# Attention and gated block in one kernel: narrowing at steps' ends, global work first, four scaling products, a packed transposition less

## The chip, the cores and the metric

The kernel runs on one core of a Trainium2 chip. The metric is the device time of one execution in microseconds (us); lower is better. The core has four compute engines that run their own instruction queues in order: TensorE (PE in the profile, PEld for its weight loads), VectorE (DVE), ScalarE (ACT) and GpSimd (POOL). SyncE (SP) issues most transfers.

## What is computed

The reference is attention, then a gated feed-forward block, then a routed block of 8 experts, all in fp32. Cut to what the change touches:

```python
# batch 4, 8 heads, 512 local and 32 global positions, head_dim 64, window 32
s_g = scale * q_g @ k_all.T            # 32 global queries see all 544 keys
out_g = sm(s_g) @ v_all
s_ll = where(|i - j| <= 32, scale * q_l @ k_l.T, -1e9)
s_l = concat([scale * q_l @ k_g.T, s_ll])   # local queries: 32 global keys and the window
out_l = sm(s_l) @ concat([v_g, v_l])
x = concat([out_g, out_l])             # 2304 tokens of 512
gate = 1 / (1 + exp(-(x @ w_gate)))    # 512 x 1536
x = (gate * (x @ w_val)) @ w_out       # then the routed experts on rows that a score picks
```

## The kernel before

**Attention** runs as a software pipeline of 38 steps over 32 units; unit u is 128 local queries (tile u // 2) of one half g = u % 2 of the heads, and a step does a different stage for several units. The list MAIN gives the order in a step u: scores of the global queries out (u-1), `turn_mm` (u-3), `normalise` (u-2), `score_mm` (u), `turned` (u-3), `x_out` (u-5), the exponentials (u-1), the middle of the step ("mid"), the scores' maxima `score_max` (u), `global_mm` (u), `value_mm` (u-4), and the end of the step ("end"). Each engine's queue is in this written order.

A unit's weights `pr` are 128 x 2 x 320: for each of two pairs of heads two chunks of 160 (128 local keys and 32 global ones). `normalise` divides by the row sums r (128 x 4) and copies the global keys' columns into a packed tile `pk`; `turn_mm` transposes four blocks of 128 and the packed one on TensorE into the tile `tp`; `turned` copies it to `pt`; `value_mm` (L438) multiplies.

**Side work** is put into the middles and ends of steps by tables of (step, stage); a half number is the middle of the step above it. `side` holds the functions for each place, called in the order in which they were put there. G_STEPS (G_LAST for the last batch) lists, from step 8b + 8, the stages of the global queries of batch b for g = 0 and 1: top (maximum), weigh (exponential, ScalarE, L463), over (reciprocal of the sums, VectorE, L467 and L468), norm (the weights `pgf`, 128 x 544, times it; its engine is ENG['g_n']), turn and turned (transposition on TensorE, L477, and copy to `ptg`, L112), value (L491, L492), out.

W_STEPS does the same for five of the twelve weight sets of the gated block. A set is three tiles of 512 KB that come as 64-bit integers: fetch (transfer to `raw`), narrow (three VectorE passes, L164, L166, L168, to fp32), total (ScalarE, L185), sum over partitions (TensorE, L188), scale (VectorE, L178 to L180 and L539), high (ScalarE, L110) and low (VectorE, L210 and L117). X_STEPS splits the tokens of the gated block's first part. W_TAIL does sets 5 and 6 in steps 33 to 36, partly; the rest is in block 0.

**Gated blocks** go over the tokens in BLOCKS of 4, 3, 3, 2, 3, 2 tiles of 128, each over 12 chunks fc of 128 columns: `up` (24 matmuls, L576 to L578), `gated` (sg on ScalarE L587, g on VectorE L589), `cut` (gh on ScalarE, go on VectorE L603) and `down` of the chunk before (L615 to L617). Block 0's first four chunks' `up` run at the ends of steps 33 to 36. Block 0 also makes weight sets 6 to 11: w1_sum, w1_make (scale, high, low, the next transfers) and w1_words (narrows and totals of a later set).

Of the kernel before, what the change touches and what calls it, by code (L numbers as in the profile page):

```python
# [49 lines left out]
G_STEPS = [[(0, 'top'), (0.5, 'weigh'), (1.5, 'over'), (1.5, 'norm'), (2, 'turn', 0), (2.5, 'turned', 0), (3, 'turn', 1), (3.5, 'turned', 1), (4, 'value'), (4.5, 'out')], [(1, 'top'), (1.5, 'weigh'), (2.5, 'over'), (2.5, 'norm'), (5, 'turn', 0), (5.5, 'turned', 0), (6, 'turn', 1), (6.5, 'turned', 1), (7, 'value'), (7.5, 'out')]]  # L50
G_LAST = [[(0, 'top'), (0, 'weigh'), (0.5, 'over'), (0.5, 'norm'), (1, 'turn', 0), (1, 'turned', 0), (1.5, 'turn', 1), (1.5, 'turned', 1), (2, 'value'), (2.5, 'out')], [(0, 'top'), (0, 'weigh'), (0.5, 'over'), (0.5, 'norm'), (2.5, 'turn', 0), (2.5, 'turned', 0), (3, 'turn', 1), (3, 'turned', 1), (3.5, 'value'), (4, 'out')]]
W_STEPS = [(0, 'fetch', 0), (0.5, 'fetch', 1), (2.5, 'narrow', 0), (3, 'total', 0), (3, 'narrow', 1), (3.5, 'fetch', 2), (3.5, 'total', 1), (4, 'sum'), (4.5, 'scale'), (4.5, 'high', 0), (5, 'low', 0), (5, 'high', 1), (5.5, 'narrow', 2), (5.5, 'low', 1), (6, 'high', 2), (6, 'low', 2)]
W_FIRST = (8, 13, 18, 23, 28)

W_TAIL = [(33.5, 'narrow', 15), (34, 'total', 15), (34.5, 'narrow', 16), (35, 'total', 16), (35, 'narrow', 17), (35, 'fetch'), (35.5, 'sum', 5), (36, 'make', 5),
# [5 lines left out]
ENG = {'x': 'a', 'g_n': 'a', 't0': 'a', 't1': 'a', 'tg': 'v'}  # L61
# [19 lines left out]
def moe_kernel(ctx, tc, qL, kL, qG, vA, wpack, epack, wr, wrT, masks, cst, out):  # L81
# [311 lines left out]
    def normalise(u):  # L393
        pr, r = U[u, "pr"], U.pop((u, "r"))
        nc.vector.tensor_scalar(r, r, 1e-9, None, op0=ALU.add)
        nc.vector.reciprocal(r, r)
        r = r.rearrange("q (a c) -> q a c", a=2).unsqueeze(3)
        (st, n), (ca, _), (one, _) = pr.ap
        x = bass.AP(tensor=pr.tensor, offset=pr.offset, ap=[[st, n], [ca, 2], [192 * one, 2], [one, 128]])
# [3 lines left out]
        nc.vector.tensor_tensor(pk.rearrange("q (a c k) -> q a c k", a=2, c=2), pr[:, :, 128:192].rearrange("q a (c k) -> q a c k", c=2),  # L403
                                r.to_broadcast([128, 2, 2, 32]), op=ALU.mult)
# [45 lines left out]
    def globals_(b, g):  # L450
# [310 lines left out]
    def w1_make(n):  # L761
# [11 lines left out]
        w1_words(n + 2 if n >= NWA else n + 1)  # L773
# [53 lines left out]
    for u in range(STEPS):  # L827
# [170 lines left out]
    for n in range(NB):  # L998
# [11 lines left out]
        for fc in range(NFC):  # L1010
            if n or fc >= EARLY:
                up(n, fc)
                gated(n, fc)
                cut(n, fc)
            if n == 0:
# [5 lines left out]
            if n == 0 and fc == 1:  # L1021
                cut(0, 3)
# [389 lines left out]
```

## Time and profile before

| | us |
|---|---|
| median of 3 runs | 815.66 (813.95 to 815.85) |
| profiled execution | 819.66 |
| its span, first to last instruction | 817.9 |
| busy in the span: TensorE / VectorE / ScalarE / GpSimd | 747.9 / 503.2 / 359.1 / 65.4 |
| mean granted clock of TensorE, share of full | 0.961 |

The span is the profiled execution's without the 1.76 us around it. Engines run beside each other, so busy times don't add up. Attention fills the first 180 us or so, the gated blocks the time to about 630 us, the experts the rest.

### The profile page before, as it was taken

What the parts mean: (1) busy time and instruction counts of PE and PEld (TensorE: products, weight loads), DVE (VectorE), ACT (ScalarE), POOL (GpSimd) and SP (SyncE); (2) the same over time, 40 slices, a digit from 0 to 9 for tenths busy, and PEclk for the clock granted to TensorE, in tenths of its full rate; (3) what the DMA queues carried; (4) which work ended last, traced back from release to release, by engine and by line L of the source; (5) the groups of instructions that cost most, each with busy time, mean ns of one, the idle gap of its engine ahead of it and who ended that gap; (6) DMA issues with size and microseconds to landing.
All of it is one profiled execution on the core that took longest, in us unless ns stands there. A gap on an engine that the chain in (4) does not pass through costs nothing. (4 is left out here: it accounts for less than half of the span.)

```text
span 817.9 us, 14475 instructions
## 1 busy us (share of the span) xinstructions
PE 747.9 (91%) x5110; PEld 560.0 (68%) x5110; DVE 503.2 (62%) x1369; ACT 359.1 (44%) x874; POOL 65.4 (8%) x92
## 2 busy tenths in 40 slices
PE   6988888998979999999999999999999866999993
PEld 5877787756545666666678866678787645777772
DVE  6768899768884277546557746336555567763731
ACT  5965887733443322132232232235334465561630
POOL 2000000000000000010010010000303112230200
PEclk9998899999999999999999999999999798999997
DMA  8999997556402210110021010015635567873300
GB/s 229 231 258 254 277 270 214 159 157 220 167 26 103 91 39 1 53 40 26 1 80 39 1 66 26 27 61 185 175 110 166 186 227 240 260 247 104 135 15 18
DMA packets 60360, 106.03 MB, mean 130 GB/s; under 512 B 9185, under 2 KB 31249, under 8 KB 60258
## 3 DMA queue, kind: packets, MB, share of 16 engines
q1 hardware_dynamic: 54242, 94.60, 37.6%
q0 software_dynamic: 3136, 6.73, 2.6%
q10 hardware_dynamic: 2880, 3.41, 1.4%
q8 instruction: 55, 0.90, 0.5%
q14 instruction: 47, 0.39, 0.2%
HBM read 87.84 MB, written 18.12 MB: 130 GB/s over the span
## 5 line engine op out<-in xcount | busy, mean ns | idle before, releaser
L576 PE MATMUL pp<-xh,wa 128*128 128x384 f16 (+2 forms) x576 | 184.3, 320 | 4.3 <-ACT sg L587 4.3
L577 PE MATMUL pp<-xl,wa 128*128 128x384 f16 (+2 forms) x576 | 183.6, 319 | 0.0
L578 PE MATMUL pp<-xh,wa 128*128 128x384 f16 (+2 forms) x576 | 183.4, 318 | 0.0
L589 DVE SCALAR_TENSOR_TENSOR g<-pp,inv,sg 128x384 f32<-128x384 f32 (+2 forms) x72 | 42.8, 594 | 100.9 <-PE pp L578 98.0
L224 DVE TENSOR_TENSOR wb<-raw,wa 128x1024 fp32r<-128x1024 f32 x64 | 76.7, 1222 | 28.7 <-ACT wa L223 27.7
L587 ACT ACTIVATE sg<-pp,inv 128x384 f32<-128x384 f32 (+2 forms) x72 | 40.4, 561 | 119.8 <-PE pp L578 113.1
L602 ACT CAST gh<-g 128x384 fp32r<-128x384 f32 (+2 forms) x71 | 35.0, 494 | 129.3 <-DVE g L589 129.3
L576 PEld LDWEIGHTS <-wa 128*128 128x128 f16 x576 | 56.9, 99 | 44.8 <-issue 16.5
L615 PE MATMUL acc<-wb,gh 128*128 128x512 f32 x200 | 86.5, 433 | 0.2 <-ACT gh L602 0.2
L577 PEld LDWEIGHTS <-wa 128*128 128x128 f16 x576 | 56.6, 98 | 33.5 <-issue 5.7
L617 PE MATMUL acc<-wb,go 128*128 128x512 f32 x200 | 79.3, 397 | 0.0
L578 PEld LDWEIGHTS <-wa 128*128 128x128 f16 x576 | 56.6, 98 | 33.1 <-issue 1.6
L616 PE MATMUL acc<-wb,gh 128*128 128x512 f32 x200 | 79.0, 395 | 0.0
L223 ACT CAST wa<-raw 128x1024 fp32r<-128x1024 f32 x64 | 65.5, 1049 | 27.1 <-DMA raw<-in_epack_dram 25.2
L725 DVE CUSTOM_DVE_ANT_0 junk<-x,wrow 128x512 f32<-128x512 f32 x108 | 75.4, 698 | 2.6
L603 DVE TENSOR_TENSOR go<-g,gh 128x384 fp32r<-128x384 f32 (+2 forms) x71 | 37.9, 534 | 39.1 <-ACT gh L602 39.1
L351 PE MATMUL sp<-k,qz 128*128 128x160 f32 x256 | 47.6, 336 | 8.0 <-DMA qz<-in_qL_dram 5.4
L391 ACT ACTIVATE pr<-sm,st 128x160 f32<-128x160 f32 x128 | 53.0, 424 | 0.0
L351 PEld LDWEIGHTS sp<-k,qz 128*128 128x128 f32 x256 | 41.8, 217 | 9.7 <-POOL tok L274 5.3
L705 POOL DMA_INDIRECT lst<-tok,pi x17 | 17.1, 1009 | 346.0 <-DVE cum L709 342.4
L615 PEld LDWEIGHTS acc<-wb,gh 128*128 128x128 f32 x200 | 37.7, 189 | 9.2 <-ACT gh L602 0.4
L617 PEld LDWEIGHTS acc<-wb,go 128*128 128x128 f32 x200 | 37.6, 188 | 9.0 <-DVE go L603 0.2
(280 smaller groups left out, 1345.3 us busy)
## 6 DMA issues: line engine op xcount, KB each, us to landing
raw<-in_epack_dram SPq DMA_DIRECT2D x64, 512.0 KB
raw<-in_wpack_dram SPq DMA_DIRECT2D x36, 512.0 KB
k<-in_kL_dram SPq DMA_DIRECT2D x32, 256.0 KB
x1d<-x SPq DMA_DIRECT2D x16, 260.0 KB
w<-in_vA_dram SPq DMA_DIRECT2D x32, 128.0 KB
xTd<-xT SPq DMA_DIRECT2D x16, 256.0 KB
out_dram<-x SPq DMA_DIRECT2D x16, 256.0 KB
v<-in_vA_dram SPq DMA_DIRECT2D x12, 256.0 KB
```

Of the source, the lines that this page charges most:

```text
L223: nc.scalar.copy(t[0], raw)
L224: nc.vector.tensor_sub(t[1], raw, t[0])
L351: nc.tensor.matmul(sp[:, 160 - 160 * s:320 - 160 * s], q, qk[t][g][:, pp, 96 * s:96 * s + 160], start=True, stop=True)
L391: nc.scalar.activation(U[u, "pr"][:, c // 2, cs], sm[:, c // 2, cs], AF.Exp, bias=st[:, c:c + 1], scale=-1.0, accum_out=U[u, "r"][:, c:c + 1])
L576: nc.tensor.matmul(pp[:, 0:nt], hi[:, ks], xh[k][:, 0:nt], start=(k == 0), stop=False)
L577: nc.tensor.matmul(pp[:, 0:nt], hi[:, ks], xl[k][:, 0:nt], start=False, stop=False)
L578: nc.tensor.matmul(pp[:, 0:nt], lo[:, ks], xh[k][:, 0:nt], start=False, stop=(k == 3))
L589: nc.vector.scalar_tensor_tensor(g[:, 0:nt], ps[1][:, 0:nt], inv[:, 2 * fc + 1:2 * fc + 2], sg[:, 0:nt], op0=ALU.mult, op1=ALU.mult)
L615: nc.tensor.matmul(acc, gh[:, gs], hi, start=(fc == 0), stop=False)
L616: nc.tensor.matmul(acc, gh[:, gs], lo, start=False, stop=False)
L617: nc.tensor.matmul(acc, go[:, gs], hi, start=False, stop=(fc == NFC - 1))
L725: nc.vector.tensor_tensor_reduce(junk, R["x1"][:, g, 0:DM], wrow[c], op0=ALU.mult, op1=ALU.add, scale=1.0, scalar=0.0, accum_out=R["lo"][: ...
```

## The change

The change moves global and weight stages to other half steps (the tables below) and puts the global stages ahead of other side work in the same place (`first=True`). The global weights are normalised on GpSimd instead of ScalarE. `normalise` uses four products of 128x160 with a per-partition scalar, in place, instead of two with a broadcast operand, and writes no packed tile; `turn_mm` turns the global keys' columns with two matmuls of 64 stationary columns against the identity instead of one packed transposition. `value` computes for each half only the 32 columns that it needs. The sum and the making of set 5 go half a step back, behind `up(0, 3)`; those of set 6 go behind `down(0, 0)`; in block 0 a set's totals and third narrow are put off (list `late`) to between `gated` and `cut` of the next chunk.

```diff
-G_STEPS = [[(0,'top'),(0.5,'weigh'),(1.5,'over'),(1.5,'norm'),(2,'turn',0),(2.5,'turned',0),(3,'turn',1),(3.5,'turned',1),(4,'value'),(4.5,'out')],
-           [(1,'top'),(1.5,'weigh'),(2.5,'over'),(2.5,'norm'),(5,'turn',0),(5.5,'turned',0),(6,'turn',1),(6.5,'turned',1),(7,'value'),(7.5,'out')]]
+G_STEPS = [[(0,'top'),(0.5,'weigh'),(1,'over'),(1.5,'norm'),(2.5,'turn',0),(3,'turned',0),(3.5,'turn',1),(4,'turned',1),(4.5,'value'),(5,'out')],
+           [(1,'top'),(1.5,'weigh'),(2,'over'),(2.5,'norm'),(5.5,'turn',0),(6,'turned',0),(6.5,'turn',1),(7,'turned',1),(7.5,'value'),(8,'out')]]
-W_STEPS = [(0,'fetch',0),(0.5,'fetch',1),(2.5,'narrow',0),(3,'total',0),(3,'narrow',1), ...
-           (5,'low',0),(5,'high',1),(5.5,'narrow',2),(5.5,'low',1),(6,'high',2),(6,'low',2)]
+W_STEPS = [(0,'fetch',0),(1,'fetch',1),(2,'narrow',0),(2.5,'total',0),(3,'narrow',1), ...
+           (5,'low',0),(5.5,'high',1),(6,'low',1),(6,'narrow',2),(6.5,'high',2),(7,'low',2)]
-W_TAIL = [... (35.5,'sum',5),(36,'make',5), ...
+W_TAIL = [... (36,'sum',5),(36.5,'make',5), ...
-ENG = {'x': 'a', 'g_n': 'a', ...
+ENG = {'x': 'a', 'g_n': 'p', ...
...
-    def at(u, f):
+    def at(u, f, first=False):
...
-            side.setdefault(u, []).append(f)
+            side.setdefault(u, []).append((not first, f))
+    def side_work(u):
+        for _, f in sorted(side.get(u, ()), key=lambda x: x[0]):
+            f()
...
-        nc.vector.tensor_tensor(x, x, r.to_broadcast([128, 2, 2, 128]), op=ALU.mult)
-        U[u, "pk"] = pk = apool.tile([128, 128], F32, tag="pk", name="pk", bufs=2)
-        nc.vector.tensor_tensor(pk.rearrange(...), pr[:, :, 128:192].rearrange(...), r.to_broadcast([128, 2, 2, 32]), op=ALU.mult)
+        for c in range(4):
+            x = pr[:, c // 2, 160 * (c % 2):160 * (c % 2) + 160]
+            nc.vector.tensor_scalar(x, x, r[:, c:c + 1], None, op0=ALU.mult)
...
-        nc.tensor.transpose(tp[:, 4], U.pop((u, "pk")), ident)
+        for pp in range(2):
+            nc.tensor.matmul(tp[64 * pp:64 * pp + 64, 4], pr[:, pp, 128:192], ident, start=True, stop=True)
...
             for pp in range(2):
-                for c in range(4):
-                    nc.tensor.matmul(xo[:, pp], v[:, c, 2 * g + pp], pt[:, c, 64 * pp:64 * pp + 64], ...)
-                nc.tensor.matmul(xo[:, pp], v[0:64, 4, 2 * g + pp], pt[0:64, 4, 64 * pp:64 * pp + 64], ...)
+                for c in range(5):
+                    k = slice(0, 128 if c < 4 else 64)
+                    for j in range(2):
+                        hs, o = slice(64 * j, 64 * j + 64), 64 * pp + SG * j
+                        nc.tensor.matmul(xo[hs, pp], v[k, c, 2 * g + pp, hs], pt[k, c, o:o + SG], ...)
...
+        def rest():
+            if n < NW:
+                for k in range(3 * n, 3 * n + 2):
+                    total_w1(k)
+                narrow_w1(3 * n + 2)
...
+                while late:
+                    late.pop()()
                 cut(n, fc)
-            if n == 0:
+            if n == 0 and fc:
                 w1_sum(W_MAKE.get(fc, NW))
...
             if n == 0 and fc == 1:
+                w1_sum(W_MAKE[0])
+                w1_make(W_MAKE[0])
                 cut(0, 3)
```

The new lines lie up to 4 further down in the attention and 1 in the gated block (L395 is L399, L467 is L468, L578 is L579).

What this moves is seen in three places of the engines' queues. The first is VectorE in the attention around step 10, where the first tile of the first weight set (step 8 on) is narrowed. In the rows, out<-in are tiles: `pr` a unit's weights, `r` its row sums, `cut` and `raw` the narrowing, `gt` the global sums, `sm` the masked scores, `ptg` the turned global weights. Before:

```order
L400 TENSOR_TENSOR pr<-pr,r 128x2x2x128
L403 TENSOR_TENSOR pk<-pr,r 128x128
L164 TENSOR_SCALAR cut<-raw 128x512
L166 SCALAR_TENSOR_TENSOR cut<-raw,cut 128x512
L168 SCALAR_TENSOR_TENSOR raw<-raw,cut 128x512
L112 COPY ptg<-tpg 128x512
L467 TENSOR_SCALAR gt<-gt 128x1
L468 RECIPROCAL gt<-gt 128x1
L362 ISA sm,st<-sp,mask_sb 128x160
```

And after the change:

```order
L468 TENSOR_SCALAR gt<-gt 128x1
L469 RECIPROCAL gt<-gt 128x1
L164 TENSOR_SCALAR cut<-raw 128x512
L166 SCALAR_TENSOR_TENSOR cut<-raw,cut 128x512
L168 SCALAR_TENSOR_TENSOR raw<-raw,cut 128x512
L399 TENSOR_SCALAR r<-r 128x4
L400 RECIPROCAL r<-r 128x4
L403 TENSOR_SCALAR pr<-pr,r 128x160 x4
L366 ISA sm,st<-sp,mask_sb 128x160
```

The narrowing (L164 to L168) stood behind the normalising and ahead of the copy to `ptg` and of `over` (L467, L468); now it stands behind `over` and ahead of the normalising and of the maxima (L362, now L366), and the copy comes a step's maxima later.

The second is VectorE in block 0, in a chunk from 4 on. `g` and `go` are the chunk's, `wa` and `wb` the low parts of a set, `cut` and `raw` the narrows of a later one. Before:

```order
L589 SCALAR_TENSOR_TENSOR g<-pp,inv,sg 128x512
L603 TENSOR_TENSOR go<-g,gh 128x512
...
L210 SCALAR_TENSOR_TENSOR wa<-raw,ws,wa 128x512 x2
L117 TENSOR_TENSOR wb<-raw,wb 128x512
L164 TENSOR_SCALAR cut<-raw 128x512 x2
L166 SCALAR_TENSOR_TENSOR cut<-raw,cut 128x512 x2
L168 SCALAR_TENSOR_TENSOR raw<-raw,cut 128x512 x2
L164 TENSOR_SCALAR cut<-raw 128x512
L166 SCALAR_TENSOR_TENSOR cut<-raw,cut 128x512
L168 SCALAR_TENSOR_TENSOR raw<-raw,cut 128x512
L589 SCALAR_TENSOR_TENSOR g<-pp,inv,sg 128x512
```

And after the change:

```order
L590 SCALAR_TENSOR_TENSOR g<-pp,inv,sg 128x512
L164 TENSOR_SCALAR cut<-raw 128x512
L166 SCALAR_TENSOR_TENSOR cut<-raw,cut 128x512
L168 SCALAR_TENSOR_TENSOR raw<-raw,cut 128x512
L604 TENSOR_TENSOR go<-g,gh 128x512
...
L210 SCALAR_TENSOR_TENSOR wa<-raw,ws,wa 128x512 x2
L117 TENSOR_TENSOR wb<-raw,wb 128x512
L164 TENSOR_SCALAR cut<-raw 128x512 x2
L166 SCALAR_TENSOR_TENSOR cut<-raw,cut 128x512 x2
L168 SCALAR_TENSOR_TENSOR raw<-raw,cut 128x512 x2
L590 SCALAR_TENSOR_TENSOR g<-pp,inv,sg 128x512
```

Of the three narrows behind the lows the third has moved into the next chunk, between `g` and `go`.

The third is TensorE at the end of step 36 and the start of block 0. `pp` is the result of `up` (here its last matmul of chunk 2, and `up` of chunk 3 where `wa` follows), `tpg` a turned block of global weights, `ws` a set's sum, `xog` the global values, `acc` the result of `down`. Before, from the last matmul of chunk 2:

```order
L578 MATMUL pp<-xh_1970,wa 128x512
L477 MATMUL tpg<-ident,pgf_107 128x128
L188 MATMUL ws<-vm,onesf 128x2
L491 MATMUL xog<-ptg,v_109 128x64 x4
L492 MATMUL xog<-ptg,v_109 128x64
...
L578 LDWEIGHTS wa
L578 MATMUL pp<-xh_1970,wa 128x512
L188 MATMUL ws<-vm,onesf 128x2
L615 MATMUL acc_2806<-wb,gh 128x512
L616 MATMUL acc_2806<-wb,gh 128x512
```

After the change, from the last matmuls of chunk 3:

```order
L578 MATMUL pp<-xl_2058,wa 128x512
L579 LDWEIGHTS wa
L579 MATMUL pp<-xh_2057,wa 128x512
L188 MATMUL ws<-vm,onesf 128x2
L616 MATMUL acc_2908<-wb,gh 128x512
L617 MATMUL acc_2908<-wb,gh 128x512
L618 MATMUL acc_2908<-wb,go 128x512
...
L617 MATMUL acc_2911<-wb,gh 128x512
L618 MATMUL acc_2911<-wb,go 128x512
L188 MATMUL ws<-vm,onesf 128x2
L616 MATMUL acc_2908<-wb,gh 128x512
```

The first `ws` is the sum of set 5: it stood ahead of `up` of chunk 3 and now stands behind it. The second `ws` in each is the sum of set 6: it stood ahead of the first `down` and now stands behind it.

## Rows read from the trace of the kernel before

**Rows 1.** Table of stretches: busy us (instructions), TensorE's granted clock, DMA share, GB/s.

```profile
16.00:30.00 14.00, 13.55 (x213) 12.21 (x213) 9.81 (x55) 12.17 (x52) 0.00 (x0) 1.00 1.08 252
30.00:151.00 121.00, 102.92 (x1342) 93.73 (x1341) 100.95 (x406) 92.55 (x323) 0.00 (x0) 0.92 0.88 247
47.68:50.68 3.00, 3.00 (x11) 2.63 (x12) 2.90 (x14) 2.70 (x8) 0.00 (x0) 0.50 1.08 324
```

**Rows 2.** TensorE's waits from 30 to 250 us: total, times, longest.

```profile
PE tpg L477 <- ACT pgf L110: 4.9, 2, 3.4
PE pp L576 <- ACT sg L587: 4.3, 2, 2.4
PE tpg L477 <- DVE ptg L112: 3.9, 3, 3.3
```

**Rows 3.** Timeline of TensorE in an early step: start, duration.

```profile
24.99 0.53 PE L374 MATMUL gp<-k,qg 128*64 128x128 f32 x8
25.34 0.32 PE L438 MATMUL xo<-pt,v 128*64 128x64 f32 x4
...
26.07 0.29 PE L438 MATMUL xo<-pt,w 128*64 128x64 f32 x4
26.19 0.29 PE L438 MATMUL xo<-pt,g 128*64 128x64 f32 x4
26.41 0.66 PE L411 MATMUL tp<-ident,pr 128*128 128x128 f32 x4
26.90 0.27 PE L412 MATMUL tp<-ident,pk 128*128 128x128 f32 x1
27.01 0.30 PE L351 MATMUL sp<-k,qz 128*128 128x160 f32 x1
```

**Rows 4.** Timeline of TensorE over a global unit's values.

```profile
110.58 1.10 PE L491 MATMUL xog<-ptg,v 128*128 128x64 f32 x8
111.61 0.43 PE L492 MATMUL xog<-ptg,v 64*128 64x64 f32 x2
111.97 1.10 PE L491 MATMUL xog<-ptg,v 128*128 128x64 f32 x8
```

**Rows 5.** Timeline of VectorE's normalising; last, VectorE's groups, 16 to 151 us.

```profile
14.84 0.69 DVE L400 TENSOR_TENSOR pr<-pr,r 128x512 f32<-128x512 f32 x1
15.44 0.29 DVE L403 TENSOR_TENSOR pk<-pr,r 128x128 f32<-128x128 f32 x1
15.64 0.32 DVE L362 CUSTOM_DVE_ANT_0 sm<-sp,mask_sb 128x160 f32<-128x160 f32 x1
...
L539 DVE TENSOR_SCALAR inv<-we,xq 128x2 f32<-128x2 f32 x4 | 0.8, 221 | 0.0
```

**Rows 6.** Timeline of VectorE and TensorE around the longest wait.

```profile
45.15 0.43 DVE L164 TENSOR_SCALAR cut<-raw 128x512 uint32<-128x512 uint32 x1 [4.16 <-DMA raw<-in_wpack_dram]
...
47.68 0.48 PE L477 MATMUL tpg<-ident,pgf 128*128 128x128 f32 x1 [3.71 <-DVE gt L467]
```

**Rows 7.** Groups of ScalarE, 16 to 200 us, and of GpSimd, whole span.

```profile
L110 ACT ACTIVATE pgf<-pgf,gt 128x544 f32<-128x544 f32 x8 | 5.9, 746 | 6.2 <-DVE gt L468 6.2
...
L1005 POOL MEMSET zrows<- 128x520 f32 x1 | 0.5, 537 | 232.5 <-DVE wa L210 232.5
```

**Rows 8.** Timeline of VectorE over one turn of block 0, with idle time before.

```profile
233.78 0.75 DVE L589 SCALAR_TENSOR_TENSOR g<-pp,inv,sg 128x512 f32<-128x512 f32 x1 [0.51 <-ACT sg L587]
235.22 0.69 DVE L603 TENSOR_TENSOR go<-g,gh 128x512 fp32r<-128x512 f32 x1 [0.69 <-ACT gh L602]
...
244.60 0.75 DVE L589 SCALAR_TENSOR_TENSOR g<-pp,inv,sg 128x512 f32<-128x512 f32 x1 [0.51 <-ACT sg L587]
```

**Rows 9.** Timeline of VectorE (scale 5) and of TensorE in block 0.

```profile
187.34 0.15 DVE L178 TENSOR_SCALAR we<-ws 128x2 f32<-128x2 f32 x1
...
188.19 0.39 PE L576 MATMUL pp<-xh,wa 128*128 128x512 f16 x1
...
195.70 0.38 PE L188 MATMUL ws<-vm,onesf 128*128 128x2 f32 x2 [2.16 <-ACT junk L185]
```

More of the change, by code (lines that the diff above doesn't have):

```diff
@@ L49 @@
 V_STEPS = [(-1, 'common')] + [(2 * i - 0.5, *x) for i in range(4) for x in (('load', i), ('shifted', 0, i), ('shifted', 1, i))]
-G_STEPS = [[(0, 'top'), (0.5, 'weigh'), (1.5, 'over'), (1.5, 'norm'), (2, 'turn', 0), (2.5, 'turned', 0), (3, 'turn', 1), (3.5, 'turned', 1), (4, 'value'), (4.5, 'out')], [(1, 'top'), (1.5, 'weigh'), (2.5, 'over'), (2.5, 'norm'), (5, 'turn', 0), (5.5, 'turned', 0), (6, 'turn', 1), (6.5, 'turned', 1), (7, 'value'), (7.5, 'out')]]
+G_STEPS = [[(0, 'top'), (0.5, 'weigh'), (1, 'over'), (1.5, 'norm'), (2.5, 'turn', 0), (3, 'turned', 0), (3.5, 'turn', 1), (4, 'turned', 1), (4.5, 'value'), (5, 'out')], [(1, 'top'), (1.5, 'weigh'), (2, 'over'), (2.5, 'norm'), (5.5, 'turn', 0), (6, 'turned', 0), (6.5, 'turn', 1), (7, 'turned', 1), (7.5, 'value'), (8, 'out')]]
 G_LAST = [[(0, 'top'), (0, 'weigh'), (0.5, 'over'), (0.5, 'norm'), (1, 'turn', 0), (1, 'turned', 0), (1.5, 'turn', 1), (1.5, 'turned', 1), (2, 'value'), (2.5, 'out')], [(0, 'top'), (0, 'weigh'), (0.5, 'over'), (0.5, 'norm'), (2.5, 'turn', 0), (2.5, 'turned', 0), (3, 'turn', 1), (3, 'turned', 1), (3.5, 'value'), (4, 'out')]]
-W_STEPS = [(0, 'fetch', 0), (0.5, 'fetch', 1), (2.5, 'narrow', 0), (3, 'total', 0), (3, 'narrow', 1), (3.5, 'fetch', 2), (3.5, 'total', 1), (4, 'sum'), (4.5, 'scale'), (4.5, 'high', 0), (5, 'low', 0), (5, 'high', 1), (5.5, 'narrow', 2), (5.5, 'low', 1), (6, 'high', 2), (6, 'low', 2)]
+W_STEPS = [(0, 'fetch', 0), (1, 'fetch', 1), (2, 'narrow', 0), (2.5, 'total', 0), (3, 'narrow', 1), (3.5, 'fetch', 2), (3.5, 'total', 1), (4, 'sum'), (4.5, 'scale'), (4.5, 'high', 0), (5, 'low', 0), (5.5, 'high', 1), (6, 'low', 1), (6, 'narrow', 2), (6.5, 'high', 2), (7, 'low', 2)]
 W_FIRST = (8, 13, 18, 23, 28)
-W_TAIL = [(33.5, 'narrow', 15), (34, 'total', 15), (34.5, 'narrow', 16), (35, 'total', 16), (35, 'narrow', 17), (35, 'fetch'), (35.5, 'sum', 5), (36, 'make', 5),
+W_TAIL = [(33.5, 'narrow', 15), (34, 'total', 15), (34.5, 'narrow', 16), (35, 'total', 16), (35, 'narrow', 17), (35, 'fetch'), (36, 'sum', 5), (36.5, 'make', 5),
           (36.5, 'narrow', 18), (36.5, 'total', 18), (36.5, 'narrow', 19), (36.5, 'total', 19), (36.5, 'narrow', 20)]
@@ L502, in globals_ @@
         for r, f, *a in (G_STEPS if b < B - 1 else G_LAST)[g]:
-            at(8 * b + 8 + r, lambda f=do[f], a=a: f(*a))
+            at(8 * b + 8 + r, lambda f=do[f], a=a: f(*a), True)
     def wtile(seq):
@@ L745, in w1_fetch @@
             w1k[0] += 1
+    late = []
     def w1_words(n):
@@ L749, in w1_words @@
             narrow_w1(3 * n, 3 * n + 1)
-            narrow_w1(3 * n + 2)
-            for k in range(3 * n, 3 * n + 2):
-                total_w1(k)
+        def rest():
[3 more added lines that the diff above has]
+                narrow_w1(3 * n + 2)
+        return rest
     def w1_sum(n, ps=None):
@@ L772, in w1_make @@
         w1_fetch(3 * n + 3)
-        w1_words(n + 2 if n >= NWA else n + 1)
+        if n >= NWA:
+            late.append(w1_words(n + 2))
+        else:
+            w1_words(n + 1)()
         if n + 1 == NW:
@@ L835, in moe_kernel @@
             if f == "mid":
-                for g in side.get(u - 0.5, ()):
-                    g()
+                side_work(u - 0.5)
             elif f == "end":
@@ L845, in moe_kernel @@
                         up(0, c)
-                for g in side.get(u, ()):
-                    g()
+                side_work(u)
             elif ok(u - a[-1]):
@@ L1029, in moe_kernel @@
             if n == 0:
-                w1_make(W_MAKE.get(fc, NW))
+                if fc:
+                    w1_make(W_MAKE.get(fc, NW))
                 if fc == 2:
-                    w1_words(NWA + 1)
+                    w1_words(NWA + 1)()
             if n + 1 < NB:
```

16 lines of the change are left out of this document (4 added, 12 removed).

## The prediction

> **What bounds the kernel now.** I read the table of stretches first. In the first attention steps TensorE is busy 13.55 of 14 us at full clock, so whatever TensorE gains or loses there is time. From 30 to 151 us (the steps of units 8 to 31, 24 of them, 121/24 = 5.04 us each) nothing is full: TensorE 102.9 of 121, VectorE 100.95, ScalarE 92.6, the transfers 0.88 of their time at 247 GB/s; the mean clock is 0.92, so 0.08 x 121 = 9.7 us of TensorE's clock weren't granted [rows 1]. This stretch is bound by how four loaded queues wait for each other. Next the list of TensorE's waits, which says for whom: the global queries' passes. Their transpositions wait 4.9 us for the normalising on ScalarE (pgf), and 3.9 us for the copy of the half before (ptg); block 0 waits 4.3 us for its sigmoid [rows 2]. One more, of 3.71 us, is for VectorE's `over` (gt L467) [rows 6]. After a wait of that size the clock falls: from 47.68 us, right behind the wait of 3.71, 3 us run at 0.50, the lower of the two levels (1.2 GHz) [rows 1, 6]. The timeline of VectorE shows why `over` was late: the narrowing of a weight tile (L164) waits 4.16 us for its raw transfer, and `over` stands behind it [rows 6].
>
> **The change, part by part.** The profiled execution took 819.66 us (span 817.9, 1.76 around it), 4.0 above the median of 815.66. The terms are differences and hold for either; I put them on the median. What no measurement tells from no change is about 0.3%, 2.4 us.
>
> *turn_mm, 32 times.* The packed transposition costs 0.11 us of TensorE (26.90 to 27.01). In its place come two fp32 matmuls of 64 stationary columns, which L438 shows as a form: its groups of four begin 0.12 apart (26.07, 26.19), 64 moving columns each, 0.03 for one, two halves side by side. With 128 moving columns, each in two passes as L374 is (8 instructions for this unit's four matmuls), that is two pairs of 0.11, 0.22. What the change adds is the changeover between 64 and 128 columns inside the step, once more there and back: the last group of L438 would end at 26.31, L411 begins at 26.41 and takes 0.49 for four of 0.11, so 0.15; L374, which changes the other way, takes 0.35 (24.99 to 25.34) for two pairs of 128 columns and two of 32, about 0.27, so 0.08 to 0.1 [rows 3]. Sum 0.22 + 0.16 + 0.09 - 0.11 = +0.36 us a step. Bounds: +0.11 if the changeovers cost nothing, +0.58 if the halves don't overlap. In the six steps up to 30 us nothing hides it: 6 x 0.36 = **+2.2**.
>
> *value, 8 times.* A global unit's values take 1.03 + 0.36 us, twice: 2.78 (110.58, 111.61, 111.97) [rows 4]. The new form has 20 matmuls of 64 columns by 32 moving, 2 passes each; 10 pairs a half, at half of L438's spacing (0.029 to 0.058 a pair, depending on whether a matmul of 32 moving columns is shorter than one of 64), plus changeovers: 1.2 to 1.65, so about -1.15 each (to -1.6). Six lie before 151 us (-6.9), two in the tail. The Trainium skill, "TensorEngine Tiling (Array Packing)", Instruction Overhead, holds that a matmul carries some 60 cycles of overhead, so that short free dimensions cost as much as a longer one; by that rule the value part takes the upper 1.65 and saves 1.1 a unit, and the rows cannot yet say, since before has no matmul of 32 moving columns.
>
> *normalise, 32 times.* The two products hold VectorE 0.80 us (14.84 to 15.64). Four of 128x160 with a per-partition scalar: the nearest row with such a scalar takes 0.222 for 128x2 elements; between it and 0.69 for 512 elements I put one at 0.30, and as consecutive products overlap by 0.09 (14.84 + 0.69 against 15.44), four take 4 x 0.30 - 4 x 0.085 = 0.86 [rows 5]. +0.06 a step, bounds 0 and +0.36. It lies beside TensorE's work where TensorE is full, and in the stretch of 121 us it is 1.4 us of VectorE.
>
> *Global normalising on GpSimd.* ScalarE loses 8 passes of 0.75 us. GpSimd, idle in the stretch, gets them; before has no such pass, only a fill of 128x520 at 0.54 [rows 7], which reads nothing. I take 0.54 as the lower bound, twice it (a read as well) as the upper: 0.5 to 1.1. Between this pass and the first transposition lies one step (5 us) for g = 0 and three for g = 1, which hides it. The tail's g = 0 has half a step, about 2.5 us.
>
> *Order in units 8 to 31.* Global work goes ahead of the narrowing, and narrowing moves to steps' ends. The waits of rows 2 that can go are 4.9 + 3.9 = 8.8 us, and most of the lost clock with them: 9.7, less 1.5 for the 3 us behind the 3.71. That 3.71 is half another matter: narrow 0 stands half a step earlier now, in front of norm(9) and the scores' maxima, so VectorE still waits for the raw tile; only `over` is no longer behind it. These 17 us are not all to be had: VectorE has 100.95 us of work, 4.2 of raw wait and 1.4 of new scaling, so at most 121 - 106.5 = 14.5. Against that: `over` now stands half a step behind `weigh`, a pass of ScalarE as long as the pgf one (0.75, some 0.95 with its handover) [rows 7], and VectorE waits for it, 6 x 0.95 = 5.7; TensorE gets 24 x 0.36 - 6.9 = +1.7; the raw wait grows by up to half a step, I take 2.1. 14.5 - 5.7 - 1.7 - 2.1 = 5.0, **-5.0** for the stretch; bounds 0 (raw transfers set the pace) and -14.
>
> *Tail, 151 to 196 us.* TensorE carries this part as it does the first steps: two value units -2.3, two or so turns +0.7: **-1.5**.
>
> *Block 0.* Two things of opposite sign. The totals and the third narrow now stand between g and go of the next chunk. One turn of the chain takes 10.82 us now (g at 233.78 and 244.60), in which VectorE waits twice: 0.51 before g, for a sigmoid that ScalarE does behind the totals, and 0.69 before go, for gh [rows 8]. With the totals gone the sigmoid comes in time, and the third narrow stands where VectorE waited for gh: a turn of 9.6. Saved 1.2 in each of 3 turns: -3.6. TensorE needs 8.4 a turn (10.82 less its longest wait for sg, 2.4 [rows 2]), so VectorE stays the bound and all of it counts. But sum 5 now stands behind up(0,3) on TensorE. Before, scale 5 began at 187.34, while up(0,3) ran from 188.19 to 195.70 - 2.16 = 193.54 [rows 9]; now it, the lows, narrows 18 to 20 and set 6 wait for up(0,3)'s end, 6.2 later; the shorter values bring that end forward by 0.4 or more, so I take 5.8. TensorE has down(0,0), about 3 us (a turn's 8.4 less up's 5.35), in the gap and then waits for total 19 about 4.9 instead of 2.16. VectorE's later idle time before block 0's turns takes up another 0.7. So the turn that restarts TensorE at 244.6 comes 5.8 - 3.6 - 0.7 = 1.5 later, and the half clock behind the 2.4 us wait, which cost some 1.7, should go with that wait: **-0.2**, bounds -5 (idle time hidden, saving and clock whole) and +4 (the reverse).
>
> Sum: +2.2 - 5.0 - 1.5 - 0.2 = -4.5: **811.2 us** (for an execution like the profiled one 815.2).
>
> **Rivals.** (1) *Most stalls go*: the stretch gives its bound of 14, as VectorE waits for `over` in time that it would idle anyway: 815.66 + 2.2 - 14 - 1.5 - 0.2 = 802.2. For it: the waits are named one by one in rows 2. Against: VectorE is 83% busy there, so a stall removed from TensorE soon meets VectorE. (2) *Nothing in the stretch*: the raw tiles set the pace. For it: 1.08 and 324 GB/s in 47.68 to 50.68 [rows 1] and the 4.16 us of rows 6, which stays. 815.66 + 2.2 - 1.5 - 0.2 = 816.2. (3) *Slower: VectorE's idle time behind sum 5 carries through.* Up(0,3) holds back scale 5, and block 0 pays +4; with nothing gained in the stretch 815.66 + 2.2 - 1.5 + 4 = 820.4. It decides as soon as the stretch gives less than 2.3. For it: the chain of VectorE from 187 to 245 us has hardly an idle microsecond to absorb 5.8. (4) *Block 0 better*: the wait behind sum 5 lies in TensorE's own cover and the saving stays: -5 there, 806.4. (5) *GpSimd's pass is slow*: it moves forward only while VectorE is idle, 17% of the stretch: 0.54 to 1.1 becomes 3.2 to 6.5 us, against 5.0 of cover for g = 0; 3 turns late by up to 2 us, 6 in all: 817.2, more with the tail. The Trainium skill, "GPSIMD Engine Reference", Specifications, says that GpSimd shares its SBUF interfaces with VectorE and contends with some forms of its instructions; no row of before shows GpSimd working beside VectorE in the attention, so this can't be weighed yet.
>
> **How the numbers follow.** Forecast 0.42 (own range 806 to 814.5), rival 1 0.14, rival 2 0.18, rival 3 0.12, rival 4 0.07, rival 5 0.07. The range of 802 to 820.5 reaches rival 1 and rival 3, and leaves out half of each and the far end of 5: about 0.17. Faster (under 813.2): 0.37 of the forecast, rivals 1 and 4 whole, 0.02 of 2: 0.60. Same: 0.05 of the forecast, 0.12 of 2, 0.04 of 3 and 5: 0.21. Slower (over 818.1): 0.04 of 2, 0.11 of 3, 0.04 of 5: 0.19.
>
> **What the profile after would show.** Steps 2 to 7 some 0.36 us longer each, from the four transpositions' end to the next L351 0.47 instead of 0.11; the values' stretch 1.2 to 1.65 instead of 2.78; four 128x160 products in 0.86; GpSimd's 128x544 pass at 0.5 to 1.1 (rival 5: over 3); TensorE's waits for pgf and ptg under 3 us together, and a new VectorE wait for ScalarE's weigh of about 1 us, six times; TensorE's wait at sum 6 about 5 us; VectorE idle before scale 5 for about 5 us; block 0's turn 9.6. I am wrong if the raw wait grows beyond half a step, if the clock stays at 0.92 although the marked waits are gone, or if block 0's turn stays above 10.

## The result and the profile after

The changed kernel takes 805.33 us (median of 4, 803.2 to 807.09) against 815.7 of before: ratio 0.9877, 95% interval 0.9847 to 0.9906, 10.4 us faster. Measured again beside the experiments the ratio was 0.9867 (0.9825 to 0.991). The forecast was 811.2 in a range of 802 to 820.5: the direction and the range hold, the gain is more than twice the one that was forecast. The time lies just under the forecast's own range of 806 to 814.5, between rival 1 (802.2) and rival 4 (806.4); the stated range reached it by way of these rivals. Single executions of one kernel lie up to 7 us from their median here, mostly by the attention and the experts, so below a time is a median and a trace is used for where, not for how much in all.

The table of stretches of the changed kernel, to be read beside [rows 1]:

```profile
16.00:30.00 14.00, 14.00 (x191) 11.41 (x191) 10.15 (x61) 11.13 (x46) 0.00 (x0) 1.00 1.08 262
30.00:151.00 121.00, 111.06 (x1624) 93.45 (x1622) 105.62 (x465) 94.11 (x336) 7.20 (x30) 0.94 0.89 247
```

In the early steps TensorE has gone from 13.55 to 14.00 of 14: it was the bound and got more to do. In the stretch of the units TensorE is busy 8 us more and VectorE 4.7 more than before in the same 121 us; that isn't all new work, since the window now reaches further into the program (unit 31 starts at 144.07 instead of 147.25). GpSimd's 7.2 are six of the passes that were ScalarE's, and the fills of `late_setup`.

TensorE's longest waits, 20 to 250 us, answer [rows 2]:

```profile
PE ws L188 <- ACT junk L185: 4.6, 1, 4.6
PE tp L410 <- ACT xh L110: 2.1, 1, 2.1
PE tp L410 <- ACT wb L110: 1.5, 1, 1.5
```

No global transposition (`tpg`) waits for `pgf` any more, and the sigmoid's 4.3 us are gone; the wait for the total of set 6, 2.2 us before, is now 4.6. VectorE's waits in the same time (the raw transfer of [rows 6], and the new one for the exponential):

```profile
DVE gt L468 <- ACT pgf L464: 3.9, 3, 1.6
...
DVE cut L164 <- DMA raw<-in_wpack_dram: 2.0, 3, 1.6
```

The new forms, on TensorE in an early step [rows 3] and in a global unit's values [rows 4], and on VectorE [rows 5]; the idle time before an instruction is in brackets:

```profile
27.41 0.66 PE L410 MATMUL tp<-ident,pr 128*128 128x128 f32 x4
28.00 0.44 PE L413 MATMUL tp<-ident,pr 128*64 128x128 f32 x4
28.37 1.35 PE L355 MATMUL sp<-k,qz 128*128 128x160 f32 x8
...
148.55 1.72 PE L495 MATMUL xog<-ptg,v 128*64 128x32 f32 x40 [0.48 <-DVE ptg L112]
150.19 0.34 PE L439 MATMUL xo<-pt,v 128*64 128x64 f32 x4
```

```profile
27.95 0.94 DVE L403 TENSOR_SCALAR pr<-pr,r 128x160 f32<-128x160 f32 x4
...
39.12 0.15 DVE L468 TENSOR_SCALAR gt<-gt 128x1 f32<-128x1 f32 x1 [1.58 <-ACT pgf L464]
```

From the first transposition to the next scores it is 0.96 us (27.41 to 28.37) where it was 0.60. The values take 1.64 (148.55 to 150.19) instead of 2.78. The four products take 0.94 instead of 0.80. In block 0 a turn of VectorE's chain takes 9.44 us where it was 10.82 (9.6 was forecast).

Lengths between the first matmuls of marked places in the traces show where the time went. "up 0" is chunk 0 of block 0, "up 3" its chunk 3; each is the start in the timeline of TensorE, in us, and the last column is the mean granted clock over all executions that were timed (61 of before, 10 of after). The second trace of after is that of its repetition below.

| trace | unit 2 to 8 | 8 to 31 | 31 to up 0 | up 0 to up 3 | up 3 to block 1 | rest | clock |
|---|---|---|---|---|---|---|---|
| before | 18.27 | 117.04 | 12.56 | 28.38 | 90.66 | 539.0 | 0.966 |
| after | 20.49 | 112.05 | 9.56 | 24.47 | 90.50 | 535.8 | 0.974 |
| after, second trace | 20.67 | 113.59 | 9.55 | 24.47 | 90.44 | 531.8 | |
| forecast of the difference | +2.2 | -5.0 | -1.5 for both | | -0.2 | 0 | |
| difference | +2.2 | -5.0 | -3.0 | -3.9 | -0.2 | -3.2 | |
| difference, second trace | +2.4 | -3.5 | -3.0 | -3.9 | -0.2 | -7.2 | |

The rest (blocks 1 to 5 and the experts) is the same code; its 3.2 and 7.2 us are differences of single executions, as the profiled one of before was 4.0 above its median and that of after 0.9 above its own. The same holds for part of the column 8 to 31, where two traces of the same code are 1.5 apart; the tail repeats to 0.01.

The marks don't cut where the forecast's sum did. From unit 8 to unit 31 are 23 steps and five units of values; the sum counted 24 steps and six units, since the sixth begins at 150.66 us in before, behind unit 31 (147.25) and ahead of 151. By the sum's own terms the forecast between these marks is -4.2 from unit 8 to 31 (one unit of 1.15 less, one turn of 0.36 less) and -2.3 from there to up 3.

### The profile page after: what moved, and what is told of

The parts are those of the page before. It is cut to its first block, busy times and chain, and to the rows that moved or that the text cites. A ratio compares the mean times of both kernels' runs of the same rounds, so it can differ in the third digit from the quotient of the medians.

```text
span 804.4 us, 15078 instructions
## 1 busy us (share of the span) xinstructions
PE 748.6 (93%) x5366; PEld 552.6 (69%) x5366; DVE 504.8 (63%) x1425; ACT 354.7 (44%) x866; POOL 72.0 (9%) x100
## 5 line engine op out<-in xcount | busy, mean ns | idle before, releaser
L579 PE MATMUL pp<-xh,wa 128*128 128x384 f16 (+2 forms) x576 | 182.6, 317 | 0.0
L578 PE MATMUL pp<-xl,wa 128*128 128x384 f16 (+2 forms) x576 | 182.6, 317 | 0.0
L616 PE MATMUL acc<-wb,gh 128*128 128x512 f32 x200 | 87.6, 438 | 0.3 <-DVE we L178 0.3
L617 PE MATMUL acc<-wb,gh 128*128 128x512 f32 x200 | 79.9, 400 | 0.0
L579 PEld LDWEIGHTS <-wa 128*128 128x128 f16 x576 | 56.3, 98 | 32.3 <-issue 0.2
L578 PEld LDWEIGHTS <-wa 128*128 128x128 f16 x576 | 56.5, 98 | 28.4
L395 ACT ACTIVATE pr<-sm,st 128x160 f32<-128x160 f32 x128 | 53.0, 424 | 0.0
```

The source lines that it names most:

```text
L395: nc.scalar.activation(U[u, "pr"][:, c // 2, cs], sm[:, c // 2, cs], AF.Exp, bias=st[:, c:c + 1], scale=-1.0, accum_out=U[u, "r"][:, c:c + 1])
L578: nc.tensor.matmul(pp[:, 0:nt], hi[:, ks], xl[k][:, 0:nt], start=False, stop=False)
L579: nc.tensor.matmul(pp[:, 0:nt], lo[:, ks], xh[k][:, 0:nt], start=False, stop=(k == 3))
L616: nc.tensor.matmul(acc, gh[:, gs], hi, start=(fc == 0), stop=False)
L617: nc.tensor.matmul(acc, gh[:, gs], lo, start=False, stop=False)
```

## The experiments

Each is the changed kernel with one part undone, or the kernel before with one part alone. The ratio is to the kernel before, timed on the same chip in turn; the changed kernel is at 0.987 to 0.988.

**Global values as before**

```diff
-                for c in range(5):  # two matmuls of 64 x 32 each
+                for c in range(4):
+                    nc.tensor.matmul(xo[:, pp], v[:, c, 2 * g + pp], pt[:, c, 64 * pp:64 * pp + 64], ...)
+                nc.tensor.matmul(xo[:, pp], v[0:64, 4, 2 * g + pp], pt[0:64, 4, 64 * pp:64 * pp + 64], ...)
```

> The changed kernel with the global values as before (10 matmuls of 128 stationary by 64 moving columns a unit and two copies out). Theory: the shorter values (2.78 to 1.64 us a unit) pay for the part between the last attention step and up(0,3), the term that my sum had too small: three units lie there, 3.4 us, and with them come back the two stretches at half clock that before had there (3.4 us); in units 8 to 31 five more units cost up to 5.7, of which about half is hidden. 813 us, 810 to 817, with clock 0.5 again somewhere between 150 and 180 us. Rival: the two half-clock stretches went because the order of the work changed, and the values only cost their own time in the tail: 808 to 809, no half clock there.

Measured: 815.38 us, ratio 1.0007 (0.9978 to 1.0036), in the theory's range and above its 813. Without the shorter values the whole gain is gone, 11 us for eight units that TensorE does 1.14 us faster each (9.1). In its trace 31 to up 0 takes 10.9 and up 0 to up 3 26.8, together 3.7 more than after: three units at 1.14 and no half clock. So the old values alone don't bring the half clock back there, as the rival said; the total is the theory's. The trace is that of the fastest of 12 executions, 6.6 us under their median, and from unit 8 to 31 it takes 112.25 us, no more than after. Where the rest of the 11 us goes in a typical execution is not shown; the mean clock over the 12 is 0.969, under after's 0.974.

**Normalising and turning as before**

```diff
-        for c in range(4):
-            nc.vector.tensor_scalar(x, x, r[:, c:c + 1], None, op0=ALU.mult)
+        nc.vector.tensor_tensor(x, x, r.to_broadcast([128, 2, 2, 128]), op=ALU.mult)
+        ...  # pk, the second product
-            nc.tensor.matmul(tp[64 * pp:64 * pp + 64, 4], pr[:, pp, 128:192], ident, start=True, stop=True)
+        nc.tensor.transpose(tp[:, 4], U.pop((u, "pk")), ident)
```

> The changed kernel with the normalising and the turning as before (two products with a broadcast operand, packed tile, one transposition of 128). Theory: the two matmuls of 64 columns cost 0.46 us of TensorE in each of 32 steps (3.66 against 3.20 in a plain step) and give nothing back, so undoing them gains 2.2 to 2.8 in steps 2 to 7, 1.4 in the tail and some 2 to 5 in units 8 to 31: 799 us, 796 to 802, faster than both kernels. Rival: in units 8 to 31 VectorE is the bound (87% busy) and nothing comes back there, or the two products cost VectorE as much as the four: 801.5 to 803.

Measured: 807.48 us, ratio 0.9897 (0.9862 to 0.9931): both theories fall. TensorE has 0.46 us less to do in each of 32 steps, 14.7 in all, steps 2 to 8 go back to 18.15 us, and yet the kernel isn't faster. The mean clock over its executions is 0.967, the same as before's on that chip. Its trace shows where it was lost, in the stretch from unit 31 to up 0, which takes 12.79 us at a clock of 0.73 (table of stretches):

```profile
142.24:155.03 12.79, 11.03 (x167) 10.03 (x166) 12.02 (x40) 9.50 (x31) 1.11 (x2) 0.73 0.53 155
```

and in TensorE's waits from 30 to 155 us, where seven waits for VectorE's `pr` lead the list:

```profile
PE tp L415 <- DVE pr L404: 13.6, 7, 4.8
```

**Sum 5 early**

```diff
-W_TAIL = [... (36, 'sum', 5), (36.5, 'make', 5), ...
+W_TAIL = [... (35.5, 'sum', 5), (36, 'make', 5), ...
```

> The changed kernel with sum 5 and make 5 in their old places (35.5 and 36), so ahead of up(0,3) on TensorE. Theory: sum 5 behind up(0,3) costs TensorE its wait of 4.60 us at sum 6 and the 6.8 us at half clock behind it (3.4 us); undone, the wait is 2 us or less at full clock and VectorE's set 5 comes some 5 us earlier: 800.5 us, 798 to 803, up(0,4) 4 to 6 us sooner after up(0,3). Rival: VectorE's chain of block 0 takes the time back (a turn of 9.6 against TensorE's 8.2), TensorE waits for sg in chunks 7 to 9 again: 804 to 806, same.

Measured: 803.37 us, ratio 0.9858 (0.9816 to 0.9899); the interval holds the changed kernel's, and the time lies between the theory's range and the rival's. The trace bears out the mechanism: TensorE's wait at sum 6 is 2.3 instead of 4.6, the half clock behind it 3.4 us long instead of 6.8, and from up 3 to block 1 it takes 87.45 us instead of 90.50. Part of it comes back at the end, where TensorE waits 1.0 for VectorE's scale: the rival's chain, but worth 1 us and not 3.

**Order as before**

```diff
-G_STEPS, W_STEPS of the changed kernel
+G_STEPS, W_STEPS of the kernel before
-            side.setdefault(u, []).append((not first, f))
+            side.setdefault(u, []).append((True, f))
```

> The changed kernel with the tables G_STEPS and W_STEPS of before and no precedence for global work (all else as changed). Theory: the order is what gained in units 8 to 31 (5.0 us there, against 1.7 more TensorE work): TensorE's waits of over 3 us for the global turns come back, and 812 us, 808 to 816. Rival: the gain there comes from the shorter values and from ScalarE's passes on GpSimd, and the order is worth nothing: 804 to 807.

Measured: 811.07 us, ratio 0.9945 (0.9913 to 0.9977). The theory's 812 fits: the order is worth some 6 us, with the other parts in place. The waits come back in its trace, from 30 to 155 us, though 8 to 31 takes only 115.87 us there (112.05 and 113.59 after), as this trace lies 3.1 us under the run's median:

```profile
PE tpg L478 <- POOL pgf L114: 4.4, 2, 3.4
PE tpg L478 <- DVE ptg L112: 4.0, 1, 4.0
```

**The changed kernel again**

> The changed kernel again, unchanged, beside the others on their chip: single executions of one kernel lie up to 6 us from its median here, and differences of under 1% need a common base. 805.3 us, 803.5 to 807, clock 0.973. Were it above 808, the readings against 805.3 would have to be redone.

Measured: 806.99 us, ratio 0.9867 (0.9825 to 0.991), clock 0.974. The chip's kernel before was at 818.36, so ratios are the common base, not microseconds.

**Old products, both ways of turning**

```diff
+        # normalise as before, with pk
         for pp in range(2):
             nc.tensor.matmul(tp[64 * pp:64 * pp + 64, 4], pr[:, pp, 128:192], ident, start=True, stop=True)
+        nc.tensor.transpose(tp[:, 4], U.pop((u, "pk")), ident)
```

> The changed kernel with the normalising and the packed transposition of before, and the two matmuls of 64 columns kept in front of the transposition, which overwrites what they wrote: TensorE does both (0.6 us a step more than with the old form alone), VectorE only the old products. Theory: TensorE's time is not what binds from unit 8 on; its additional work fills waits, and with TensorE more evenly occupied the clock is granted more often (the old form alone: 0.967, the changed kernel 0.973). So 807.5 us, 805 to 809.5, clock 0.971 or more, steps 2 to 7 at 20.5 us or more. Rival: TensorE's work counts, and the old form alone only looked slow for its placing: 32 x 0.5, 812 to 820, clock still 0.967.

Measured: 810.11 us, ratio 0.9905 (0.987 to 0.9939), clock 0.975. Beside the run with the old turning alone (0.9897) it differs in nothing but the two matmuls, and its ratio is the same. They make the time from the transpositions to the scores 1.12 us instead of 0.60, 0.52 a step or 16.6 in all (0.6 a step was expected). The mean clock is 0.975 against 0.967. The same two views show what took them in, though in the fastest of 8 executions (804.46): the stretch from unit 31 to up 0 is 9.63 us at full clock,

```profile
143.78:153.41 9.63, 9.22 (x174) 7.69 (x174) 9.22 (x32) 7.99 (x28) 0.00 (x0) 1.00 0.49 138
```

and the waits for `pr` shrink from 13.6 to 4.9 us:

```profile
PE tp L415 <- DVE pr L404: 4.9, 7, 1.2
```

**The new values alone**

```diff
 # the kernel before, with value() and out_() of the changed kernel
```

> The kernel before with the new global values alone (20 matmuls of 64 by 32 a unit, one copy out). Theory: the values are the larger part of the whole gain (undone in the changed kernel they cost 10.0 us): 806.5 us, 804 to 809. Rival: the values count only where the order leaves TensorE the bound; in the old order the waits for the global turns stay and swallow five of eight: 810 to 813.

Measured: 809.89 us, ratio 0.9897 (0.9856 to 0.9937), some 8.4 us, beside a kernel before at 818.36: the theory, whose 806.5 was a ratio of 0.989. The clock stays low (0.9645). Its trace is that of the slowest of six executions (815.31), and is used below for the clock in the tail alone.

**The global normalising on ScalarE**

```diff
-ENG = {'x': 'a', 'g_n': 'p', ...
+ENG = {'x': 'a', 'g_n': 'a', ...
```

> The changed kernel with the global weights' normalising on ScalarE again. Theory: 8 passes of 0.75 us come back to an engine that is 78% busy in the stretch, in the middle of steps; TensorE's waits for pgf return in part: 807.5 us, 805.5 to 811. Rival: GpSimd and VectorE slow each other (a GpSimd pass of 0.98 instead of 0.72, a VectorE narrowing pass of 1.09 instead of 0.69 beside it), and ScalarE has room: 803 to 805.3.

Measured: 809.94 us, ratio 0.9883 (0.9839 to 0.9926), against 0.9867 of the changed kernel on the same chip. Inconclusive: 1.3 us between the ratios and 3.0 between the medians, with intervals of 3 each way. No wait of a global transposition for `pgf` returns in its trace, so that part of the theory falls; 8 to 31 takes 116.68 us there, 3 to 4.6 more than in the two traces of after, which one trace can't settle.

**Block 0's words at once**

```diff
-        if n >= NWA:
-            late.append(w1_words(n + 2))
-        else:
-            w1_words(n + 1)()
+        w1_words(n + 2 if n >= NWA else n + 1)()
```

> The changed kernel with block 0's totals and third narrow at once again, behind the lows of the same chunk. Theory: VectorE's turn goes back from about 9.5 to 10.8 us in three turns, TensorE waits for sg again at chunks 7 and 8 (some 4 us) and the clock may fall there once: 3 to 6 us more than the changed kernel, 0.9915 of before (0.989 to 0.995), up(0,4) to up(0,9) 45 us instead of 41.5. Rival: the sum behind up(0,3) has left TensorE so late that VectorE's longer turn is hidden: within 1 us of the changed kernel, 0.987.

Measured: 811.44 us, ratio 0.9955 (0.9926 to 0.9983), a loss of some 6 to 7 us against the changed kernel, more than the 3 to 6 of the theory. In the trace 4.3 of them lie between up 3 and block 1 (94.79 us instead of 90.50), where TensorE's waits from 180 to 275 us are:

```profile
PE ws L188 <- ACT junk L185: 4.6, 1, 4.6
PE pp L577 <- ACT sg L588: 3.7, 3, 2.4
```

Both waits stand here, the new one for total 19 and the old one for the sigmoid; the changed kernel has only the first.

**Three stages moved**

```diff
-W_TAIL: (36, 'sum', 5), (36.5, 'make', 5)        G_STEPS: (1, 'over'), (1.5, 'norm') and (2, 'over'), (2.5, 'norm')
+W_TAIL: (35.5, 'sum', 5), (36, 'make', 5)        G_STEPS: (1.5, 'over'), (2, 'norm') and (2.5, 'over'), (3, 'norm')
-            if n == 0 and fc == 1:  # sum and make of set 6
+            if n == 0 and fc == 2:
```

> The changed kernel with three stages moved: sum 5 and make 5 early (35.5 and 36, ahead of up(0,3)), sum and making of set 6 one down later, and the global over and norm half a step later (1.5 and 2, 2.5 and 3), so that VectorE no longer waits for the exponential. Theory: the waits of 4.6 us at sum 6 and of 3.9 us on VectorE go, with the half clock behind the first: 0.982 of before (0.978 to 0.986). Rival: as in the run with the early sum alone, VectorE's chain and the raw transfers take most of it back: 0.985 to 0.988, no different from the changed kernel.

Measured: 804.4 us, ratio 0.9873 (0.9833 to 0.9913): the rival. In the trace TensorE doesn't wait between up 3 and up 4, but then 1.7 us at the next sum and 2.2 in three waits for VectorE's scale, so VectorE's chain takes it back (88.30 us from up 3 to block 1, against 87.45 with the early sum alone). VectorE's wait for the exponential is gone, but its wait for raw transfers is 5.9 us, where after has 2.0 and 3.5. No run here beats the changed kernel by more than the uncertainty.

**More work for TensorE in the kernel before**

```diff
+        for pp in range(2):
+            nc.tensor.matmul(tp[64 * pp:64 * pp + 64, 4], pr[:, pp, 128:192], ident, start=True, stop=True)
         nc.tensor.transpose(tp[:, 4], U.pop((u, "pk")), ident)
```

> The kernel before with two matmuls of 64 columns put ahead of the packed transposition, which overwrites what they write; everything else as before. About 0.57 us more for TensorE in each of 32 steps, 18 us in all, and no other engine does more. Theory: outside steps 2 to 7 (2 to 3 us) TensorE has room, and more even work keeps the clock up: no half clock between the last attention step and up(0,3), mean clock from 0.965 to 0.972; the time is 0.996 to 1.005 of before. Rival: TensorE's work is paid in full or in large part: 1.010 to 1.022.

Measured: 818.99 us, ratio 1.0058 (1.0024 to 1.0091), clock 0.972 over 12 executions where before has 0.966 over 23. The step is 0.52 us longer on TensorE, so of 16.6 us of work 4.7 are paid (2.0 to 7.4). That is just above the theory's range and below the rival's. In its trace 2.2 us more are spent in steps 2 to 8 and 4.0 more from unit 8 to 31, a third of the work there, so the theory's room is not for all of it; 2.6 come back from unit 31 to up 3. The table of stretches from unit 31 to up 0 and on to up 3, for before, for this kernel and for the changed one, shows the clock (the last column but two):

```profile
147.25:159.81 12.56, 10.92 (x146) 9.57 (x145) 10.31 (x35) 8.25 (x30) 0.00 (x0) 0.86 0.43 113
159.81:188.19 28.38, 27.24 (x198) 16.91 (x194) 16.89 (x39) 12.31 (x24) 0.00 (x0) 0.94 0.52 159
```

```profile
153.81:165.28 11.47, 10.37 (x153) 8.72 (x153) 9.40 (x31) 8.12 (x30) 0.00 (x0) 1.00 0.42 117
165.28:192.14 26.86, 25.95 (x201) 16.17 (x198) 16.87 (x39) 12.30 (x24) 0.00 (x0) 1.00 0.56 167
```

```profile
144.07:153.63 9.56, 9.08 (x173) 7.68 (x172) 9.17 (x35) 7.76 (x28) 0.00 (x0) 1.00 0.55 154
153.63:178.10 24.47, 23.67 (x238) 13.63 (x234) 15.83 (x36) 10.82 (x21) 1.42 (x2) 1.00 0.49 143
```

With nothing but useless matmuls added the first stretch takes 11.47 us instead of 12.56 and the second 26.86 instead of 28.38, both at full clock.

## Why the prediction was right in direction and short in size

**Steps 2 to 8, +2.2.** Right: 20.49 against 18.27 us, 20.67 in the second trace, and 18.15 with the old turning. The form's price was right too: +0.36 from the transpositions to the scores, and 0.1 more on the scores behind it.

**The stretch, -5.0.** The direction and the order's share are right: the run with the old order gives back 6 us, with the waits. That the first trace shows just -5.0 is in part luck: the second shows -3.5, and between the marks the sum's own terms give -4.2. Its parts were partly off. VectorE's wait for the exponential is 3.9 us (2.7 in the second trace) and not 5.7. The raw wait, for which I added 2.1, fell from 5.0 to 2.0 (3.5). And rival 1, most stalls go, had its mechanism and not its time: the waits for `pgf` are gone, and TensorE is idle 9.9 of 121 us where it was 18.1; what is left is mostly other waits, from 30 to 155 us 5.5 us for ScalarE and 3.4 for VectorE. Half clock is left too: 13.6 us of it from 30 to 151, where before had 20.4.

**The tail, -1.5.** This term failed: between the marks it was -2.3 and measured -6.9 (12.56 to 9.56 and 28.38 to 24.47), the same in both traces of after. Its three units of values are worth 3.4 us; before ran 6.8 us of it at half clock, from 153.1 and from 177.0 us, which cost another 3.4, and after has none; TensorE's waits in it went from 2.8 to 1.3; and three turns at 0.46 cost 1.4. Together -6.9. The step that was wrong is "TensorE carries this part as it does the first steps": it priced the tail at full clock and without waits, and before had neither. Of before there is one trace, 4.0 us above its median, so how much half clock a typical execution has there is not shown; the mean clocks (0.966 and 0.974) go the same way.

The clock is the part of the tail that I hadn't thought of at all. It didn't fall back with the old values or with the old order: with the old form of either it is full there too. What goes with it is the two matmuls of 64 columns. The ten traces here that have them show no half clock between unit 31 and up 3, the three without (before, the old turning, the new values alone) each show some, and the mean clocks over all executions agree in both pairs that differ in nothing else: 0.967 and 0.975 in the changed kernel, 0.966 and 0.972 in the one before. How the additional work keeps the clock up no run shows.

**turn_mm as a cost.** So the sum also mis-sized this term, with its 2.2 us early, 8.6 in the stretch and 0.7 in the tail. TensorE's additional 0.36 us a step is paid in the first six steps; later it fills time in which TensorE waits for VectorE's `pr` (13.6 us of waits without it, 4.9 with it), and the clock is granted for more of the time. Undone, it gains nothing (0.9897 against 0.987). It isn't free everywhere: in the kernel before, a third of such work is paid from unit 8 to 31. I had said that the clock at 0.92 belongs to the stalls; it rose to 0.94 in the stretch and to 1.00 in the tail, and by the mean clocks more by TensorE's own work (0.972 with that alone) than by the stalls' end (0.967 with all but that).

**value.** The price of 1.15 us a unit was right (1.14). That rule about the overhead of a short matmul, which the Trainium skill states in "TensorEngine Tiling (Array Packing)", Instruction Overhead, agrees with the trace: 40 instructions of 32 columns in 1.64 us are 0.041 each, with the changeovers in it, where those of 64 columns take 0.03 without [rows 3]. That is the end of the forecast's range that took no gain from fewer columns; 20 pairs at its 0.058 are 1.16, which leaves 0.48 for changeovers; at its 0.029 the same working gives 1.06, so the lower end of 1.2 was not what the terms give. What the sum got wrong is that it set six of the eight units against the turning's 8.6; they are worth 8.4 us alone and 11 in the changed kernel, more than TensorE's 9.1.

**Block 0, -0.2.** Right in sum (90.66 to 90.50). Undone in the traces, the deferred words are worth 4.3 us there (forecast 3.6) and the sum behind up(0,3) costs 3.0, where I had 5.1 less 1.7 for the clock; the two leave -1.3, so a microsecond of this term is not accounted for by either alone. The turn came out (9.44 us, forecast 9.6), and the half clock behind the wait for the sigmoid is gone, as I had said. TensorE's wait at sum 6 is 4.60 (forecast 4.9), and behind it stands 6.8 us of half clock that I had not foreseen. VectorE's scale of set 5 and TensorE's matmuls around it:

```profile
183.61 0.16 DVE L178 TENSOR_SCALAR we<-ws 128x2 f32<-128x2 f32 x1 [2.65 <-PE ws L188]
...
183.83 0.50 PE L616 MATMUL acc<-wb,gh 128*128 128x512 f32 x1 [0.25 <-DVE we L178]
...
191.49 0.58 PE L188 MATMUL ws<-vm,onesf 128*128 128x2 f32 x2 [4.60 <-ACT junk L185]
...
192.50 0.63 PE L617 MATMUL acc<-wb,gh 128*128 128x512 f32 x1
```

VectorE waits 2.65 us for the sum, not the 5 that I gave it, since the cut of chunk 2 and a copy out kept it until 181. Against the start of up 3 (178.10) scale 5 begins 5.5 us after, where it began 0.85 ahead [rows 9]: 6.4 later, for which I took 5.8. The matmul at 192.50 takes 0.63 where the one at full clock takes 0.39.

**The other rivals.** Nothing in the stretch (2) and slower (3) are refuted by the marks of the table. Block 0 better (4) is what the early sum shows to be open, by 3 us in the trace. GpSimd's slow pass (5) is refuted: 0.72 us.

## What to carry to other kernels

A stage of TensorE that sits between waits can be given work for less than its length, here 4.7 us for 16.6, and taking work out of it can win nothing: price it by the wait that ends last there, and look at the granted clock of the stretch in both profiles before a term is written as so many steps times so much. Set the marks by which a result will be read before the sum is made, and cut the sum there: a unit that lies between two bounds can make a wrong term look right. The parts aren't additive: undone one at a time, the values, the order and the deferred words come to 11, 6 and 6 to 7 us, of a gain of 10.4 in all. Why is not shown.

## What was not expected of the hardware

GpSimd's pass and some of VectorE's instructions are slower beside each other. Timeline of VectorE and GpSimd of the changed kernel, at two of the passes:

```profile
43.24 0.98 POOL L114 TENSOR_SCALAR pgf<-pgf,gt 128x544 f32<-128x544 f32 x1
43.67 1.09 DVE L166 SCALAR_TENSOR_TENSOR cut<-raw,cut 128x512 uint32<-128x512 uint32 x1
44.80 0.69 DVE L168 SCALAR_TENSOR_TENSOR raw<-raw,cut 128x512 uint32<-128x512 uint32 x1
...
86.75 0.72 POOL L114 TENSOR_SCALAR pgf<-pgf,gt 128x544 f32<-128x544 f32 x1 [4.53 <-PE sp L355]
86.86 1.15 DVE L210 SCALAR_TENSOR_TENSOR wa<-raw,ws,wa 128x512 f16<-128x512 f32 x1 [0.30 <-ACT wa L110]
```

The narrowing pass with two tile operands (L166) takes 1.09 us beside GpSimd's pass and 0.69 elsewhere, the low part (L210) 1.15 instead of 0.75, and GpSimd's own pass 0.98 instead of 0.72, once in eight passes. The maximum over 544 columns keeps its 0.70 beside a pass. The Trainium skill, "GPSIMD Engine Reference", Key points, says that GpSimd shares its SBUF interfaces with VectorE and contends with instructions that have two SBUF inputs or run in a 2-port perf mode. The rows of L166 and L210, with two inputs, agree: 0.4 us each, three times in the stretch of this trace. In the second trace L164, with one input, takes 0.80 instead of 0.42 beside a pass; in which mode it runs no view shows. Nor was it expected that useless matmuls could shorten a stretch: unit 31 to up 3 takes 40.94 us in before, at clocks of 0.86 and 0.94, and 38.33 with more work in it at full clock.
